# RetNet attention and a gated feed-forward layer on one core: the order of work at the entry of token tile 1, and transposing transfers for chunks 14 to 16

## The chip, the core and the metric

One core of a Trainium2 chip. It has TensorE (PE; its weight loads are shown apart as PEld), VectorE (DVE), ScalarE (ACT), GpSimd (POOL), and SyncE (SP), which here only issues transfers. Sixteen DMA engines move data. PE writes to PSUM, the accumulation memory; DVE and ACT bring results from there to SBUF, the working memory. The metric is device time of one launch in microseconds, the median of several runs; lower is better.

## The reference

Shapes: q, k, v are [8 batches, 8 heads, 576 positions, 64], the feed-forward layer has 4608 tokens (8 x 576), width 512 and 2048 hidden units.

```python
scores = matmul(q, k.T) / sqrt(64)
gamma = 1 - 2 ** (-5 - head)
D[i, j] = gamma ** (i - j) if i >= j else 0
x = matmul(scores * D, v)                 # then [8*576, 512]
h = x @ w_in                              # 512 -> 2048
g = h * tanh(softplus(h))                 # Mish
out = g @ w_out                           # 2048 -> 512
```

## The kernel before

**Chunks and tiles.** The 576 positions of a batch are cut into four chunks of 128 and a rest of 64; two rests make one chunk. There are 36 chunks of 128 tokens. Chunks 0 to 7 are the first 128 positions of the eight batches; 8 to 14 belong to batches 0 and 1 (14 is their two rests), 15 to 21 to batches 2 and 3, and so on. Four chunks make a token tile (t), nine in all. `g1(t, f)` makes 128 of the 2048 hidden units for a tile: four products of 128x512 over `w_in_t` and `xT`, then a Mish activation on ACT into `gT`. `g2(t, i)` does four of the 16 products of one output chunk; `store` copies the result to `res` (DVE or ACT) and SP sends it out.

**Attention.** Decay is put into q, k and v ahead of the products. For a chunk n, `step_p` (P) scales and casts q and k into `qks` on DVE (two instructions of 128x512), `step_v` (V) does the same for v, `step_t` (T) transposes `qks` into `qkT`. For n under NT = 16, T is eight PE transposes into PSUM and copies by ACT; from chunk 16 on it is a transposing transfer (`dma_start_transpose`, L348) on SP's queue, mostly told by `behind` to wait for PE's newest product. `load` brings a chunk's raw q, k and v (`qkraw`, `vraw`) by POOL's queue, into five and seven buffers. `visit(n)` does the rest for the pair n, n+1: states for the next pair (`states`, read from `qks` and `vs`), outputs of this pair (`outputs`, `outputs_end`, which reads `qkT` and the states' cast `ssb`), the next pair's scores (`step_s`, reads the next pair's `qkT`), two casts of `xT` (ACT and DVE, L505), and the masked scores (`step_m`, DVE). State sums are run on DVE a little later (`run(sums)`), their cast to `ssb` on ACT (`run(casts)`).

**The first two tiles** (chunks 0 to 7) go another way, without states: `f_transpose`, `f_scores`, `f_v` (cast of v to `vb`), `f_out` (products, then casts into `xT`). For tile 1 these steps lie among the 16 steps of `g2_first`, the second product of tile 0; `steps` (L712) says at which step T, S, V and O are issued. `vpair` is the raw v of two batches.

**The order** is written out by hand: each engine runs its instructions as the code issues them. The loop over `u` (24 steps) does tile 1's `g1` (steps 0 to 15) and half of its `g2` (16 to 23), with the attention steps of chunks 8 to 13 at the steps that `ps`, `vs` and `ts_` name, and visits to chunks 8 and 10. Then comes the loop over t = 2 to 9 and i = 0 to 15, in which n is the pair visited and w = i % 8 the step; pair 12 is visited at t = 2, i = 6, pair 14 at i = 14. `gated` makes the loads of chunks 17 and 18 wait for an activation of tile 2, `more_loads` makes 19 and 20 wait for PE's newest product. `halved` says for how many of the next products that neither open nor close a sum the 512 columns are done as two products of 256 (L547).

Of the kernel before, what the change touches and what calls it, by code (L numbers as in the profile page):

```python
# [16 lines left out]
def kernel(  # L17
# [21 lines left out]
    P = 128  # L39
# [4 lines left out]
    KC = d_model // P  # L44
    NCH = 4
    NPE = 18
    NT = 16
    NV = 20
    PF = 5

# [10 lines left out]
    N0 = 2 * NCH  # L61
# [38 lines left out]
    fst = {}  # L100
# [71 lines left out]
    xts = {}  # L172
# [65 lines left out]
    def f_out(t, b, copy):  # L238
        if b == 0:
            xts[t] = xp.tile([P, KC, NCH * P], BF16, name="xT")  # L240
        vb = fst[t]["vb"][b]
        if t == 0:
            pool, name = ((ps_h, "hp"), (ps_h, "hp"), (ps_st, "st"), (ps_o, "ops"))[b]
            ot = pool.tile([P, NP, P], F32, name=name)
        else:
            if b % 2 == 0:
                fst[1]["out"] = ps_sc.tile([P, 2, NP, P], F32, name="sc")
            ot = fst[1]["out"][:, b % 2]
        for p in range(NP):
            for e in range(2):  # L250
                nc.tensor.matmul(ot[ds(64 * e, 64), p, :], lhsT=vb[:, 2 * p + e, :],
                                 rhs=fst[t]["sm", b][:, 2 * p + e, :],
                                 start=(p == 0), stop=True, skip_group_check=True)
        if t == 0:
            copy(xts[t][:, :, ts(b, P)], ot)
        elif b % 2:
            for x in range(2):
                copy[x](xts[1][:, :, ts(b - 1 + x, P)], fst[1]["out"][:, x])  # L258

    def f_state(b):  # L260

# [67 lines left out]
    newest = [None]  # L329

    def step_t(n, gate=None):
        flat = live[n]["qks"].rearrange("p i h d -> p (i h d)")
        qk = tr.tile([P, 2, NP, P], BF16, name="qkT", bufs=6)
        if n < NT:
            if n in (N0 + 2, N0 + 4):
# [55 lines left out]
    def written(products):  # L391
        sync = mybir.DependencyInfo(mybir.DependencyClass.Sync, mybir.DependencyReason.DATA)
        seen = nc.sync.nop()
        for ins in products:
            tc.add_manual_dep(seen.ins, ins.ins.name, sync, reason="row halves and a bank")
        return seen
# [64 lines left out]
    def run(jobs, *how):  # L461
        while jobs:
            jobs.pop()(*how)
# [49 lines left out]
    def visit(n, banks, copies, between=None):  # L513


        units, early = states(n + 2)
        if units:
            units[0]()
        both = outputs(n, banks)
        seen = written(outputs_end(n, both, 0))  # L520
        if units:
            step_s(n + 2)
        elif between:
            between()
        for unit in units[1:early]:
            unit()
        outputs_end(n, both, 1, seen)
        for unit in units[max(early, 1):]:
            unit()
        outputs_copy(n, both, copies)  # L530
        if units:
            step_m(n + 2)

    outs = {}
    halved = [0]
    gated = {(2, 0): 17, (2, 1): 18}

# [99 lines left out]
    def att(n, steps):  # L639
        if n >= n_chunks:  # L640
            return
        for step in steps:
            {"P": step_p, "V": step_v, "T": step_t}[step](n)

    dve, act, pool = nc.vector.tensor_copy, nc.scalar.copy, nc.gpsimd.tensor_copy
# [63 lines left out]
        g1(0, f)  # L709
    for i in range(2):  # L710
        f_mix(0, i)
    steps = {0: "T0", 3: "S0 C1", 9: "T1", 11: "S1", 12: "V0 V1 V2 V3", 15: "O0 O1 O2 O3"}  # L712
    for i in range(nF):
        for step in steps.get(i, "").split():
            n = int(step[1])
            if step[0] == "T":
                for j in range(2):
                    f_transpose(1, n, j, [(ps_sc, "sc", (dve, act)[j])])
            elif step[0] == "S":
                f_scores(1, n)  # L720
            elif step[0] == "V":
                f_v(1, n, dve if n == 3 else act)
            elif step[0] == "C":
                for j in range(2):
                    f_mix(n, j)
            else:
                f_out(1, n, (dve, act))
        g2_first(i // 4, i % 4)

    queued = [4 * NCH]  # L730
# [1 line left out]
    def more_loads(upto, gate=None):  # L732
        for _ in range(2):
            if queued[0] <= upto:
                load(queued[0], gate)
                queued[0] += 1


    ps = {0: 0, 4: 1, 8: 2, 11: 3, 18: 5}
    vs = {0: 0, 5: 1, 9: 2, 13: 3, 18: 4, 19: 5}  # L740
    ts_ = {3: 0, 7: 1, 12: 2, 14: 3, 19: 4, 21: 5}
    for u in range(24):
        j, w = divmod(u, 4)
        halved[0] = 2 if 0 < u < 5 else 0
        if u in ps:
            att(N0 + ps[u], "P")
        if u == 11:
            step_m(N0)
        if u in vs:
            att(N0 + vs[u], "V")  # L750
        if w == 0 and j > 0:
            if j < 5:
                load(N0 + j + 3)
            else:
                load(N0 + j + 3)
                queued[0] += 1
        if u == 10:
            units, early = states(N0)
            seen = written(units[0]())
            step_s(N0)  # L760
            units[1]()
            units[2](seen)
            run(sums)
        elif u == 16:
            att(N0 + 4, "P")
        elif u == 17:
            visit(N0, ((ps_o, "ops"), (ps_h, "hp")), (act, act))
            run(sums)
        elif u == 22:
            visit(N0 + 2, ((ps_h, "hp"), (ps_h, "hp")), (act, dve))  # L770
        if u == 20:
            stores(act)
        if u in (13, 20):
            run(casts, dve if u == 13 else act)
        if u in ts_:
            att(N0 + ts_[u], "T")
        stores()
        if u < nF:
            g1(1, u, 2 if u == 0 else 1)
            flush()  # L780
        else:
            g2(1, u - nF)
# [3 lines left out]
    for t in range(2, nT + 1):  # L786
        for i in range(nF):
            n, w = NCH * (t + 1) + i // 8 * 2, i % 8
            if w == 2 and n in cast_at:
                cast_k0(cast_at[n])  # L790
            if w == 2:
                run(casts, act)
                halved[0] = {14: 16, 20: 29}.get(n, 0)
            if w == 6 and n < n_chunks:
                visit(n, ((ps_h, "hp"), (ps_h, "hp")), (act, dve), lambda: g2(t - 1, i))
            if w == 0:
                stores(act if n == N0 + 4 else dve)
                run(sums)
            if w == 7 and n + 2 == NPE:
                stores()  # L800
            if w in (0, 1) and n + 2 < NT:
                att(n + 2 + w, "P")
            if w in ((3, 4) if n + 2 < NPE else (0, 1)):
                att(n + 2 + (w in (1, 4)), "V")
            if w in ((4, 7) if n + 4 <= NPE + 2 else (4, 5)) and n + 4 >= NT:
                stores()
                att(n + 4 + (w != 4), "P")
            if w == 7 and NT <= n + 4 <= NPE + 2:
                step_t(n + 5, newest[0])
            if w in (1, 3) and n + 2 == NT:  # L810
                more_loads(n + 5 + w // 3, newest[0])
            if w == 1 and n + 2 == NPE:
                more_loads(n + 5, newest[0])
            if w == 1 and NPE < n + 2 < n_chunks:
                hold(n + 2)
            if w == 1 and n + 2 >= NPE:
                more_loads(n + 7)
                if t in (3, 4):
                    load_k0(2 * t - 2 + i // 8)
            if w in (4, 5) and n + 2 < NT:  # L820
                att(n - 2 + w, "T")
            stores()


            if t == 2:
                if w == 6:
                    g2(1, 8 + i // 2)
                g1(t, i)
                if w == 6:
                    step_t(n + 4, newest[0])  # L830
                if i % 2 and w != 7:
                    g2(1, 8 + i // 2)
            elif t == nT:
                if i < 12:
                    g2(t - 1, i)
            elif w == 6:

                last = n < n_chunks <= n + 2
                g2(t - 1, i + last)
                g1(t, i)  # L840
                if NPE < n + 4 < n_chunks:
                    for x in ((4, 5) if n + 4 > NPE + 2 else (4,)):
                        step_t(n + x, newest[0])
            elif w == 7 and n < n_chunks <= n + 2:
                g1(t, i)
            elif i % 4 == 0:
                g1(t, i)
                g1(t, i + 1)
                g2(t - 1, i)
            else:  # L850
                if i % 4 != 1:
                    g1(t, i)
                g2(t - 1, i)
# [32 lines left out]
```

## Time and profile before

| what | value |
|---|---|
| median of 3 runs | 299.06 us (298.16 to 299.23) |
| profiled execution, its own time | 297.8 us |
| span of the program in it | 296.1 us |
| busy: PE, DVE, ACT, POOL | 289.9, 140.2, 129.8, 124.9 us |
| transposing transfers (L348) | 20, median 3.2 us from issue to landing |
| loads of raw q, k, v of 256 KB (POOL) | 72, median 6.0 to 6.1 us from issue to landing |

Times in the profile are microseconds from the start of the span. A row of the chain of waits gives a start, a duration and what took it; a row of the timeline gives start, duration, engine, line, operation, tiles and shapes, and in brackets how long the engine stood idle before it and for whom it waited. A row of the list of waits gives total, times and longest. A row for one tile or line gives the minimum, median and maximum duration in ns and the first and last start.

### The profile page before, as it was taken

How to read it: one execution, taken by the hardware profiler on the slowest of the kernel's cores; microseconds unless marked ns; L12 is line 12 of the kernel's file. 1: busy time of each engine (PE TensorE's matmuls, PEld its weight loads, DVE VectorE, ACT ScalarE, POOL GpSimd, SP SyncE). 2: the span in 40 equal slices, each digit the busy share in tenths (PEclk: the TensorE clock that was granted, in tenths of full speed). 3: DMA queues.
4: the chain of work that ended last, by engine and by line, in shares of the span. 5: the costliest groups of instructions: out<-in, count | busy, mean ns of one | idle time of the engine just before them, and what ended most of it. 6: DMA issues, size and time to landing. Idle time of an engine off the chain costs nothing.

```text
span 296.1 us, 7921 instructions
## 1 busy us (share of the span) xinstructions
PE 289.9 (98%) x3479; PEld 156.3 (53%) x3479; DVE 140.2 (47%) x253; ACT 129.8 (44%) x213; POOL 124.9 (42%) x163
## 2 busy tenths in 40 slices
PE   7899999999999999999999999999999999999996
PEld 3556886556456545457645454545454544444443
DVE  6851547497955828454555454535454222010011
ACT  4867126775566534443353534343434433433200
POOL 8945756656427096738392727283020000000000
DMA  7999999999679999798877868686313111010132
GB/s 157 222 202 205 205 239 216 344 222 210 188 164 191 191 227 225 194 238 202 205 201 186 209 137 213 137 205 146 78 54 90 38 38 42 32 35 35 56 88 71
DMA packets 41956, 46.92 MB, mean 158 GB/s; under 512 B 23873, under 2 KB 31041, under 8 KB 41921
## 3 DMA queue, kind: packets, MB, share of 16 engines
q0 software_dynamic: 15120, 31.20, 49.5%
q1 hardware_dynamic: 26656, 15.01, 20.5%
q8 instruction: 27, 0.44, 0.7%
q10 hardware_dynamic: 144, 0.20, 0.2%
q14 instruction: 9, 0.07, 0.1%
HBM read 37.75 MB, written 9.44 MB: 159 GB/s over the span
## 4 chain that ended last, share of the span: by engine, by line
PE 83%; DMA 11%; POOL 3%; DVE 1%; issue 0%; ACT 0%; POOLq 0%; DVEq 0%
PE hp L542 39%; PE ops L542 31%; DMA w_out_t<-in_moe_w_out_dram 4%; DMA vpair<-in_v_dram 4%; DMA w_in_t<-in_moe_w_in_dram 3%; PE hp L547 2%; PE ops L547 2%; PE sc L362 1%; PE hp L493 1%; PE sc L417 1%; PE hp L476 1%; PE hp L623 1%; POOL gT L107 1%; POOL w_in_t L87 1%; PE sc L340 1%; POOL gT L118 1%
## 5 line engine op out<-in xcount | busy, mean ns | idle before, releaser
L542 PE MATMUL hp<-xT,w_in_t 128*128 128x512 bf16 (+1 forms) x539 | 131.0, 376 | 0.7 <-ACT xT L258 0.7
L579 ACT ACTIVATE gT<-hp 128x512 bf16<-128x512 f32 x142 | 84.8, 598 | 94.3 <-PE hp L542 93.5
L542 PE MATMUL ops<-w_out_t,gT 128*128 128x512 bf16 x424 | 104.7, 379 | 0.0
L542 PEld LDWEIGHTS <-w_in_t 128*128 128x128 bf16 x542 | 52.8, 98 | 56.9 <-issue 1.5
L542 PEld LDWEIGHTS <-gT 128*128 128x128 bf16 x478 | 45.5, 98 | 52.2
L631 DVE COPY res<-ops 128x512 f32<-128x512 f32 x28 | 19.3, 690 | 85.2 <-PE ops L542 85.2
L319 DVE TENSOR_TENSOR qks<-qkraw,gqk 128x512 bf16<-128x512 f32 x56 | 36.8, 711 | 2.7 <-DMA qkraw<-in_k_dram 2.7
L297 POOL DMA_DIRECT2D qkraw<-in_q_dram x24 | 21.5, 894 | 17.7 <-PE hp L542 6.3
L326 POOL TENSOR_TENSOR vs<-vraw,gv 128x512 bf16<-128x512 f32 x16 | 16.8, 1069 | 20.1 <-PE hp L476 20.0
L505 DVE CAST xT<-hp 128x512 bf16<-128x512 f32 x13 | 9.0, 692 | 31.6 <-PE hp L493 31.6
L297 POOL DMA_DIRECT2D qkraw<-in_k_dram x24 | 21.4, 891 | 3.9 <-DMA vraw<-in_v_dram 2.1
L297 POOL DMA_DIRECT2D vraw<-in_v_dram x24 | 21.2, 883 | 1.4 <-DMA w_out_t<-in_moe_w_out_dram 0.9
L505 ACT CAST xT<-hp 128x512 bf16<-128x512 f32 x14 | 8.2, 586 | 28.2 <-PE hp L493 28.2
L547 PEld LDWEIGHTS <-gT 128*128 128x128 bf16 x164 | 15.8, 98 | 3.3
L368 DVE TENSOR_TENSOR sm<-sc,mask 128x1024 bf16<-128x1024 f32 x14 | 17.0, 1216 | 0.8 <-PE sc L362 0.8
L453 DVE TENSOR_TENSOR total<-sc,total 128x256 f32<-128x256 f32 x40 | 16.9, 422 | 1.0
L511 POOL COPY held<-qkT 128x1 bf16<-128x1 bf16 x8 | 1.5, 188 | 33.4 <-DMA qkT<-qks 33.4
L456 ACT CAST ssb<-total 128x768 bf16<-128x768 f32 (+3 forms) x13 | 11.6, 894 | 2.9 <-DVE total L453 2.9
L542 PE MATMUL hp<-w_out_t,gT 128*128 128x512 bf16 x52 | 12.7, 379 | 0.0
L547 PE MATMUL hp<-xT,w_in_t 128*128 128x256 bf16 x74 | 12.0, 273 | 0.0
L547 PE MATMUL ops<-w_out_t,gT 128*128 128x256 bf16 x80 | 10.4, 273 | 0.0
L547 PEld LDWEIGHTS <-w_in_t 128*128 128x128 bf16 x76 | 7.4, 98 | 5.4 <-issue 0.2
(130 smaller groups left out, 246.1 us busy)
## 6 DMA issues: line engine op xcount, KB each, us to landing
out_dram<-res SPq DMA_DIRECT2D x31, 256.0 KB, 2.8
qkraw<-in_q_dram POOLq DMA_DIRECT2D x24, 256.0 KB, 6.0
qkraw<-in_k_dram POOLq DMA_DIRECT2D x24, 256.0 KB, 6.0
vraw<-in_v_dram POOLq DMA_DIRECT2D x24, 256.0 KB, 6.1
w_out_t<-in_moe_w_out_dram POOLq DMA_DIRECT2D x4, 512.0 KB, 11.8
gT<-in_k_dram POOLq DMA_DIRECT2D x8, 128.0 KB, 6.4
gT<-in_v_dram POOLq DMA_DIRECT2D x2, 512.0 KB, 6.8
w_in_t<-in_moe_w_in_dram POOLq DMA_DIRECT2D x2, 512.0 KB, 10.8
```

The costliest lines, as they stand in the source:

```text
L87: nc.gpsimd.dma_start(out=w_in_t[:, cs, ds(f0, n)], in_=w_in_r[:, cs, ds(f0, n)])
L297: ins = nc.gpsimd.dma_start(out=t, in_=src[b, :, ds(P * c, P), :].rearrange("h p d -> p h d"))
L319: nc.vector.tensor_tensor(slots[:, :, y], heads[:, :, y], factors[:, :, y].unsqueeze(3).to_broadcast([P, NP, 2, D]), op=OP.mult)
L326: engine.tensor_tensor(vs, live[n]["v"], gv[:, c, :].unsqueeze(2).to_broadcast([P, H, D]), op=OP.mult)
L368: nc.vector.tensor_tensor(sm.rearrange("p e x n i -> p (e x n) i"), live[n]["sc"].rearrange("p e x n i -> p (e x n) i"), mask.unsqueeze(1) ...
L453: nc.vector.tensor_tensor(new[:, k], st[:, j, x], total[b], op=OP.add)
L456: casts.append(lambda copy: copy(lows[:, 0:k], new[:, 0:k]))
L505: copy(xts[t][:, :, ds(P * s, 2 * P)].rearrange("p h (x j i) -> p j h x i", x=2, j=2)[:, j], both[j])
L542: newest[0] = nc.tensor.matmul(to, lhsT=w, rhs=x, start=first, stop=last)
L547: nc.tensor.matmul(to[:, ts(j, n)], lhsT=w, rhs=x[:, ts(j, n)], start=False, stop=False, skip_group_check=True)
L579: done = nc.scalar.activation(gts[t][:, f, :], hp, AX.Mish)
L631: copy(ot, ops)
```

## The change

In tile 1 the casts of v for batches 2 and 3 are issued at step 15, just ahead of the output products, and not at step 12 with the other two. The four casts of `xT` (128x512, DVE and ACT by turns) become two of 128x1024: ACT takes batches 0 and 1, DVE takes 2 and 3.

NT becomes 14, so chunks 14 and 15 are no longer transposed by PE and ACT but by transfers, as is 16. Their P and T move ahead: chunk 14 has P at u = 21 and T at u = 22, behind the visit; chunk 15 has both at u = 23; chunk 16 has both at i = 1 of tile 2 (before: P at i = 4, T at i = 6). None of the three waits for a product of PE. Chunk 17's stay at i = 7. The loads of chunks 17 and 18 wait for the activations of f = 2 and 3 of tile 2 and not of 0 and 1; those of 19 and 20 are issued at i = 10 and 12 and not at 9 and 11. From i = 2 of tile 2 on, 16 more products are done in halves. SP's queue gets two transfers more; POOL's order is the same.

```diff
-    NT = 16
+    NT = 14
...
         elif b % 2:
-            for x in range(2):
-                copy[x](xts[1][:, :, ts(b - 1 + x, P)], fst[1]["out"][:, x])
+            copy(xts[1].rearrange("p h (b i) -> p b h i", i=P)[:, ds(b - 1, 2)], fst[1]["out"])
...
-    gated = {(2, 0): 17, (2, 1): 18}
+    gated = {(2, 2): 17, (2, 3): 18}
...
-    steps = {0: "T0", 3: "S0 C1", 9: "T1", 11: "S1", 12: "V0 V1 V2 V3", 15: "O0 O1 O2 O3"}
+    steps = {0: "T0", 3: "S0 C1", 9: "T1", 11: "S1", 12: "V0 V1", 15: "V2 V3 O0 O1 O2 O3"}
...
-                f_out(1, n, (dve, act))
+                f_out(1, n, (act, dve)[n // 2])
...
-    ps = {0: 0, 4: 1, 8: 2, 11: 3, 18: 5}
+    ps = {0: 0, 4: 1, 8: 2, 11: 3, 18: 5, 21: 6, 23: 7}
...
             visit(N0 + 2, ((ps_h, "hp"), (ps_h, "hp")), (act, dve))
+            att(N0 + 6, "T")
+        elif u == 23:
+            att(N0 + 7, "T")
...
-                halved[0] = {14: 16, 20: 29}.get(n, 0)
+                halved[0] = {12: 16, 14: 16, 20: 29}.get(n, 0)
...
-            if w in (0, 1) and n + 2 < NT:
-                att(n + 2 + w, "P")
...
+            if n == 12 and w == 1:
+                att(n + 4, "PT")
-            if w in ((4, 7) if n + 4 <= NPE + 2 else (4, 5)) and n + 4 >= NT:
+            if w in ((4, 7) if n + 4 <= NPE + 2 else (4, 5)) and (n > 12 or w == 7):
                 stores()
                 att(n + 4 + (w != 4), "P")
-            if w == 7 and NT <= n + 4 <= NPE + 2:
+            if w == 7 and n + 4 <= NPE + 2:
                 step_t(n + 5, newest[0])
-            if w in (1, 3) and n + 2 == NT:
-                more_loads(n + 5 + w // 3, newest[0])
+            if w in (2, 4) and n + 4 == NPE:
+                more_loads(n + 5 + w // 4, newest[0])
...
-            if w in (4, 5) and n + 2 < NT:
-                att(n - 2 + w, "T")
...
-                if w == 6:
+                if w == 6 and n > 12:
                     step_t(n + 4, newest[0])
```

## The prediction

> **What bounds the kernel now.** I read the page's busy shares and chain first, then the chain of waits, in order of time, around the places that the diff touches, and then the timeline of each engine there.
>
> ```profile
> span 296.1 us, 7921 instructions
> PE 289.9 (98%) x3479; PEld 156.3 (53%) x3479; DVE 140.2 (47%) x253; ACT 129.8 (44%) x213; POOL 124.9 (42%) x163
> PE 83%; DMA 11%; POOL 3%; DVE 1%; issue 0%; ACT 0%; POOLq 0%; DVEq 0%
> ```
>
> PE is busy for 98% and carries 83% of the chain; the other engines are under half. So a microsecond counts only if PE waits for it or works in it. The list of waits has one wait of PE for another engine after the start:
>
> ```profile
> PE hp L542 <- ACT xT L258: 0.7, 1, 0.7
> ```
>
> It is the entry into tile 1, and the chain shows what stands before it:
>
> ```profile
> 32.47 12.47 DMA vpair<-in_v_dram
> ...
> 45.06 0.43 DVE vb L233
> 45.49 1.20 DVE res L631 x2
> 46.68 0.61 DVE xT L258
> ...
> 47.32 0.59 ACT xT L258
> ...
> 48.55 0.81 PE hp L542 x5
> ...
> 50.99 0.45 PE sc L340 x8
> ```
>
> The load of v for batches 6 and 7 lands at 44.94 (32.47 + 12.47). DVE then makes vb of batch 3, copies two finished rows of results that were queued behind it, casts a first row quarter of xT, ACT casts the next, and only then does PE begin tile 1. From there on PE has a fixed stream of work: what is taken out of it, or what lets it begin earlier, moves the end.
>
> **Part 1, the order in tile 1.** V2, V3 move from step 12 to step 15, and four xT casts of 128x512 become one of 128x1024 on ACT (batches 0, 1) and one on DVE (batches 2, 3). The timeline there (start, duration, engine, line):
>
> ```profile
> 41.72 2.36 DVE L226 TENSOR_TENSOR sm<-sc,dmask 128x1024 bf16<-128x1024 f32 x2 [1.45 <-PE sc L219]
> ```
> ```profile
> 45.02 0.62 ACT L233 CAST vb<-vpair 128x512 bf16<-128x512 f32 x1 [1.48 <-DMA vpair<-in_v_dram]
> 45.54 0.58 ACT L631 COPY res<-hp 128x512 f32<-128x512 f32 x1
> ```
> ```profile
> 44.90 0.38 PE L542 MATMUL ops<-w_out_t,gT 128*128 128x512 bf16 x1
> 45.20 1.12 PE L251 MATMUL sc<-sm,vb 128*64 128x128 bf16 x32
> 46.26 0.83 PE L547 MATMUL st<-w_out_t,gT 128*128 128x256 bf16 x6
> ...
> 47.95 1.41 PE L542 MATMUL hp<-xT,w_in_t 128*128 128x256 bf16 x9 [0.65 <-ACT xT L258]
> ```
> ```profile
> L205 DVE COPY qkT<-sc x2: 1225/1225/1225, 29.6 to 39.0; 128x1024 bf16<-128x1024 bf16 x2
> L205 ACT COPY qkT<-sc x2: 1012/1012/1012, 30.0 to 39.5; 128x1024 bf16<-128x1024 bf16 x2
> ```
>
> After the change: DVE is free at 44.08 and does the first result row at once; the second starts when its products end (44.90 + 0.38 = 45.28) and holds DVE for 0.60 (1.20 for two) before the next; V3 comes third, 45.93 to 46.36. ACT copies its result row before 45.02, does V2 from 45.02 to 45.64 as now, and the first pair's cast from about 45.9 (O0 and O1 are the first half of the 45.20 row) to 46.9 by the 1.01 us row. On PE, O2 runs at 45.65, O3 waits for V3 until 46.42, runs 0.24 (a quarter of 1.06, the distance from 45.20 to 46.26) and leaves 0.1 for the change of shape, then the seven products on st, which last 0.87 (six halves of 0.109 and one of 0.216, rows below): 47.64. The first half of g1(1,0) then needs no wait and goes at 47.64 instead of 47.95. The second half waits for DVE's pair: O3 done and visible at 46.9, plus 1.23, is 48.15 against 48.55 now. Gain 0.40, and about 0.1 more because the first activation of tile 1 is no longer behind a late result copy: 0.5. Bounds: 0 if the wait merely moves to O3, and 0.98 if all that PE stands there goes (47.13 to 47.95, and 0.16 ahead of 48.55). DVE ends its casts at 48.1 against 47.9, so chunk 8's scaling starts 0.2 later; its reader, the transposes at 50.99 (then 50.5), leaves more than a microsecond.
>
> **Part 2, chunks 14 to 16.** PE loses 16 transposes; 16 products get a second half.
>
> ```profile
> 80.98 0.45 PE sc L340 x8
> ...
> 82.29 0.45 PE sc L340 x8
> ...
> 86.64 3.45 PE hp L542 x16
> ...
> 139.31 1.53 PE ops L547 x14
> ```
>
> The transposes cost PE 0.45 + 0.45 = 0.90 on the path, with products on both sides. A product is 3.45/16 = 0.216, a half 1.53/14 = 0.109: two halves cost 0.218, so 16 products cost 0.04 more. PE's instruction count stays the same. Net 0.86. ACT loses two 1.01 us copies, which nothing waited for: nothing gained.
>
> The row prices a 128-column transpose at 56 ns. The Trainium skill ("TensorE: Matmul & The Clock Gate", section on sustained spacing) gives about 81 ns per matmul at N = 128 in a stream with weight loads; by that the removed work would be 1.30 and the time 0.4 lower. The trace does not agree (0.45 for eight), so the row is used.
>
> What must now be on time. P14 and P15 move to steps 21 and 23, P16 and T16 to the second step of tile 2:
>
> ```profile
> 71.14 1.29 DVE L326 TENSOR_TENSOR vs<-vraw,gv 128x512 bf16<-128x512 f32 x2
> 74.08 0.69 DVE L505 CAST xT<-hp 128x512 bf16<-128x512 f32 x1 [1.65 <-PE hp L493]
> 74.69 1.22 DVE L368 TENSOR_TENSOR sm<-sc,mask 128x1024 bf16<-128x1024 f32 x1
> 75.82 1.33 DVE L453 TENSOR_TENSOR total<-sc,total 128x256 f32<-128x256 f32 x3
> ...
> 77.53 2.49 DVE L319 TENSOR_TENSOR qks<-qkraw,gqk 128x512 bf16<-128x512 f32 x4
> ```
>
> P14 (half of 2.49, 1.25) fits the 1.65 that DVE stands idle before the cast at 74.08. P15 goes between sm and the sums and pushes these by 1.25, to 77.0 less the 0.5 of part 1; their cast for ACT then starts near 78.0, ends at 78.8, just when ACT's next activation is due (79.29 less 0.5). Cost nothing, with no slack; without that cover it would be tenths. The transfers:
>
> ```profile
> DMA to landing us min/median/max: 3.0/3.2/6.6
> ```
> ```profile
> 89.58 10.89 SPq L348 DMA_TRANSPOSE qkT<-qks  x2
> ```
> ```profile
> L362 PE MATMUL sc<-qkT x32: 186/194/194, 84.9 to 85.2; 64*64 64x64 bf16 x32
> ```
> ```profile
> L362 PE MATMUL sc<-qkT x32: 186/194/194, 96.6 to 96.9; 64*64 64x64 bf16 x32
> ```
>
> T14 is issued at about 73.2, T15 after P15 at 76.7. Both are first read in the visit to chunks 12 and 13, now at 84.9, then at 83.5: T15 has 6.8 and needs 3.0 to 6.6. On SP's queue the next store stands behind T15's wait, some 1.3 us; result tiles have four buffers, so nobody waits. T16 goes at 79.8 instead of after 87 and is read at 95.2, as is T17. The loads of 17 and 18 wait for two more activations, those of 19 and 20 for one more step:
>
> ```profile
> 77.95 0.88 POOL L297 DMA_DIRECT2D qkraw<-in_q_dram  x1 [5.89 <-ACT gT L579]
> ...
> 89.53 0.88 POOL L297 DMA_DIRECT2D qkraw<-in_q_dram  x1 [6.32 <-PE hp L542]
> ```
> ```profile
> 87.99 1.28 DVE L319 TENSOR_TENSOR qks<-qkraw,gqk 128x512 bf16<-128x512 f32 x2
> ```
> ```profile
> DMA to landing us min/median/max: 5.2/5.8/6.2
> ```
> ```profile
> DMA to landing us min/median/max: 8.9/9.8/12.4
> ```
>
> (The last two are the raw loads issued from 77.9 to 83 and from 34 to 58.) Load 17 starts 12 products later, 77.95 + 2.59 - 0.5 = 80.0, its k part at 80.9, landing at 86.1 to 87.1. P17, on DVE at 87.99 now, is due at 86.6: at most 0.5 late. T17 follows at 88.2 to 88.7; with 3.0 to 6.6 it lands at 91.2 to 95.3, for a use at 95.2. Today's T17 is issued at 89.58, 0.05 after load 19 began; then load 19 begins at 89.53 + 1.73 - 1.4 = 89.9, so T17 has over a microsecond alone. I take it as on time. POOL has nothing but later loads behind these waits.
>
> **Sum.** -0.50 - 0.90 + 0.04 = -1.36, against the profiled execution's 297.8 (span 296.1): 296.4. The median of the runs shown is 299.06, 1.26 above it; carried over, 297.7. PE's stream after 48 us is fixed, so I put the 1.26 mostly ahead of it, into the loads. If v lands d later, today's second half of g1(1,0) slips by d; in the new order V3 slips only once d passes 0.87 (46.36 against 45.49 + d). The gain of part 1 then grows to 1.3. Between 0.5 and 1.3 I take 0.65: 297.5.
>
> **Rivals.**
> 1. Tile 1 gives nothing, because O3 and the longer casts eat it, and PE enters the second half at 48.5 as now. For it: DVE's single cast is 1.23 long and starts after V3. Time: 299.06 - 0.86 = 298.2.
> 2. Slower: load 17's landing decides. P17, its transfer and the visit at 95.2 hang on it. With a landing time of 9.3 (rows: 5.2 to 6.2 there, 8.9 to 12.4 when the queue was deep) k is there at 90.2, T17 is issued at 91.8 and lands at 98.4 by 6.6: PE stands 3.2, time 300.7; with 12.4, 303.8. It costs something from 6.2 on if T17 takes its longest, and turns the sign once PE stands 1.6. For it: T16 now shares the engines with these loads. Against: the highest row there is 6.2.
> 3. T15 is late at 83.5, for loads 15 and 16 still land beside T14. From a landing time of 6.8 on each microsecond is one of PE; at 10 it is 3.2, time 300.7. Against: 6.6 is the maximum of 20. The Trainium skill ("VectorE: DVE Perf Modes", rules for kernel authors) prefers TensorE for a 128x128 transpose where PSUM will do, 390 ns against 1309 ns by DMA, which speaks against this part; taken one after the other, eight such would take an estimated 10.5 us and give this rival. The trace shows 3.0 to 6.6 for all eight.
>
> **How the numbers follow.** A change under 0.5% (1.5 us) is about what can't be told from none. Forecast with its own range 296.9 to 298.2: 0.60, of which 0.43 lie under 297.56 (faster) and 0.17 within. Rival 1: 0.17, the same. Rival 2: 0.15, of which 0.10 slower (over 300.56) and 0.05 the same, stalls that only eat the gain. Rival 3: 0.08, 0.06 slower, 0.01 the same, 0.01 still faster. Faster 0.44, same 0.40, slower 0.16. The range reaches from 296.4 (299.06 less 1.3 and 0.86, less half of the 1.07 between the highest and the lowest run shown) to 299.6 (no change, and the same half more), which leaves out the 0.16 of the slower cases.
>
> **What would show it.** Right: xT casts of 128x1024, one on ACT, one on DVE, side by side; PE's second half of tile 1 near 48.1; no L340 group at 81 and 82; halves of 0.109 in their place; the visits that stand at 84.4 and 96.1 now begin 1.4 earlier with no wait of PE in front of the qkT reads. Wrong: PE or its weight loads waiting for the transfer of qks into qkT, P17 on DVE waiting for the load of k, ACT's cast of the sums holding up an activation, or a longer standstill of PE between O2 and O3 than 0.5.

## The result, and the profile after

The changed kernel takes 297.27 us (median of 16 runs, 297.08 to 298.65); the kernel before, timed beside it, 298.64 (16 runs, 298.00 to 299.23). The ratio is 0.9962, with a 95% interval from 0.9952 to 0.9971: 1.13 us less (0.87 to 1.43). The forecast was 297.5.

The profiled execution of the changed kernel happens to be the slowest of its runs, 298.65: everything in it starts late, so its times are compared here from a common point and not from the start of the span. Lines behind 257 have a number one lower than before (L541 is the old L542). The head of the page, with the shares of the chain by engine:

```profile
span 296.9 us, 7883 instructions
PE 286.4 (96%) x3440; PEld 157.0 (53%) x3479; DVE 140.9 (47%) x252; ACT 128.2 (43%) x210; POOL 124.4 (42%) x163
PE 89%; DMA 6%; issue 2%; POOL 1%; DVE 0%; POOLq 0%
```

PE still carries the chain. Of its 3479 matmuls 39 have no record here (the weight loads are all there); each leaves a hole in the rows below, "issue" of 0.05 behind a half and of 0.16 behind a whole product. They aren't waits.

**Tile 1.** The chain of waits of the changed kernel (start, duration, what), and the timeline of PE and rows of L257:

```profile
46.55 0.23 PE ops L541
46.78 0.02 issue
46.80 0.07 DVE res L630
46.87 0.54 issue
47.41 0.43 DVE vb L233
47.84 0.04 issue
47.88 0.41 PE sc L251 x8
48.29 0.76 PE st L546 x6
49.05 0.05 issue
49.11 1.32 PE hp L541 x9
```
```profile
46.69 0.86 PE L251 MATMUL sc<-sm,vb 128*64 128x128 bf16 x24
47.88 0.41 PE L251 MATMUL sc<-sm,vb 128*64 128x128 bf16 x8 [0.33 <-DVE vb L233]
```
```profile
L257 ACT CAST xT<-sc x1: 1012/1012/1012, 47.4 to 47.4; 128x1024 bf16<-128x1024 f32 x1
L257 DVE CAST xT<-sc x1: 1225/1225/1225, 48.3 to 48.3; 128x1024 bf16<-128x1024 f32 x1
```

The output products begin at 46.69, 1.49 later than before (45.20). V3 is held by DVE's second result copy, which waits for PE's product; O3 then waits for V3; after that PE goes on with no wait over 0.1, and the 0.65 before the first half of `g1(1,0)` is gone. That first half begins 2.42 after the first output product (before: 47.95 - 45.20 = 2.75), the second half, inside the group of nine, at 49.62, 2.93 after it (before 3.35).

**Chunks 14 to 16.** The chain of the two kernels at the visits to chunks 10 and 12, before and after:

```profile
72.77 0.25 PE sc L417 x16
...
84.46 0.15 PE st L417 x2
```
```profile
74.12 0.25 PE sc L416 x16
...
79.74 0.22 PE hp L541
79.96 0.44 PE hp L546 x4
...
84.96 0.15 PE st L416 x2
```

From visit to visit it was 11.69 and is 10.84: 0.85 less. The transposes at L340 (now L339) are gone there, halves stand in their place. The transfers of chunks 14 to 17 (issued from 75.1 to 89.8) and the q, k, v loads issued from 81.9 to 91.8 landed in time:

```profile
L347 SPq DMA_TRANSPOSE qkT<-qks x4: 1240/1292/1363, 75.1 to 89.8; - x4
DMA to landing us min/median/max: 4.8/5.1/5.5
```
```profile
DMA to landing us min/median/max: 4.5/7.1/7.3
```

Their readers stand at 85.6 and 97.3, and no wait of PE or of its weight loads for `qkT` is in the list.

**What was not in the sum: the end.** The last store, and the first and last drain of SP's queue behind it (before, then after):

```profile
293.54 0.33 SPq L627 DMA_DIRECT2D out_dram<-last  x1
...
L881 SPq DRAIN  x3: 7/7/13, 295.2 to 295.5; - x3
```
```profile
294.04 0.33 SPq L626 DMA_DIRECT2D out_dram<-last  x1
...
L881 SPq DRAIN  x3: 7/7/13, 296.1 to 296.4; - x3
```

From the issue of the last store to the drain it was 1.7 and is 2.1. The store takes the same 1.54 to land. Between lie SP's waits for the completion semaphores of the transfers, one after another, about 0.06 each. An instruction of this kind has its record when its wait has ended; the starts of these records:

```
before  store lands 295.08; waits end at 293.92 293.97 294.03 294.10 294.16 294.22 294.28 294.77 | 295.10 295.16, drain 295.22
after   store lands 295.58; waits end at 294.42 294.47 | 295.60 295.66 295.72 295.78 295.84 295.90 295.96 296.02, drain 296.09
```

Before, the last store holds up the ninth of ten waits, and one is left when it has landed. After, it holds up the third, and seven are left. From landing to drain that is 0.14 against 0.51. In all 14 profiles of this study it is 0.14 without the new transfers and 0.51 with them: a fixed 0.37 that part 2 loses again. That two transfers more on SP's queue move the last store to another semaphore of a rotating set is the reading that fits; the set itself isn't in the profile.

**And a scatter that both kernels have.** In the visit to chunk 8 PE stands between products with nothing to wait for:

```profile
67.57 0.14 PE sc L361 x17
67.71 0.16 issue
67.88 0.32 PE sc L361 x15
```

From the last product before to the first after, 0.36 are lost here, 0.07 before, and 0.77 in a second profile of the changed kernel; experiments 11 and 12 come back to it.

### The profile page after: what moved, and what is told of

Its sections match the earlier page's. It is cut to its first block, busy times and chain, and to the rows that moved or that the text cites. A ratio compares the mean times of both kernels' runs of the same rounds, so it can differ in the third digit from the quotient of the medians.

```text
span 296.9 us, 7883 instructions
## 1 busy us (share of the span) xinstructions
PE 286.4 (96%) x3440; PEld 157.0 (53%) x3479; DVE 140.9 (47%) x252; ACT 128.2 (43%) x210; POOL 124.4 (42%) x163
## 4 chain that ended last, share of the span: by engine, by line
PE 89%; DMA 6%; issue 2%; POOL 1%; DVE 0%; POOLq 0%
PE hp L541 40%; PE ops L541 30%; PE hp L546 5%; PE ops L546 4%; DMA w_in_t<-in_moe_w_in_dram 3%; DMA gT<-in_v_dram 3%; PE sc L361 1%; PE hp L492 1%; PE sc L416 1%; PE hp L475 1%; PE hp L622 1%; PE st L546 1%; POOL gT L107 1%; PE st L416 1%; PE sc L339 1%
## 5 line engine op out<-in xcount | busy, mean ns | idle before, releaser
L541 PE MATMUL hp<-xT,w_in_t 128*128 128x512 bf16 (+1 forms) x512 | 127.6, 376 | 1.0 <-DMA w_in_t<-in_moe_w_in_dram 0.2
L541 PE MATMUL ops<-w_out_t,gT 128*128 128x512 bf16 x403 | 99.9, 379 | 2.0 <-issue 1.9
L541 PEld LDWEIGHTS <-w_in_t 128*128 128x128 bf16 x534 | 52.0, 98 | 55.4 <-DMA w_in_t<-in_moe_w_in_dram 1.2
L541 PEld LDWEIGHTS <-gT 128*128 128x128 bf16 x470 | 44.8, 98 | 51.3
L546 PEld LDWEIGHTS <-gT 128*128 128x128 bf16 x180 | 17.3, 98 | 3.6
L546 PE MATMUL hp<-xT,w_in_t 128*128 128x256 bf16 x90 | 14.4, 273 | 0.0
L546 PE MATMUL ops<-w_out_t,gT 128*128 128x256 bf16 x96 | 12.4, 273 | 0.2
L546 PEld LDWEIGHTS <-w_in_t 128*128 128x128 bf16 x92 | 9.0, 98 | 6.3 <-issue 0.2
L541 PE MATMUL hp<-w_out_t,gT 128*128 128x512 bf16 x49 | 12.0, 379 | 0.2 <-issue 0.2
## 6 DMA issues: line engine op xcount, KB each, us to landing
w_out_t<-in_moe_w_out_dram POOLq DMA_DIRECT2D x4, 512.0 KB, 11.8
```

The source lines that it names most:

```text
L541: newest[0] = nc.tensor.matmul(to, lhsT=w, rhs=x, start=first, stop=last)
L546: nc.tensor.matmul(to[:, ts(j, n)], lhsT=w, rhs=x[:, ts(j, n)], start=False, stop=False, skip_group_check=True)
```

## The experiments

Each kernel was run beside the kernel before on the same chip; the ratio is to that kernel. All compute the whole result.

**1. The order alone (part 1).** The kernel before with:

```diff
-            for x in range(2):
-                copy[x](xts[1][:, :, ts(b - 1 + x, P)], fst[1]["out"][:, x])
+            copy(xts[1].rearrange("p h (b i) -> p b h i", i=P)[:, ds(b - 1, 2)], fst[1]["out"])
...
-    steps = {0: "T0", 3: "S0 C1", 9: "T1", 11: "S1", 12: "V0 V1 V2 V3", 15: "O0 O1 O2 O3"}
+    steps = {0: "T0", 3: "S0 C1", 9: "T1", 11: "S1", 12: "V0 V1", 15: "V2 V3 O0 O1 O2 O3"}
...
-                f_out(1, n, (dve, act))
+                f_out(1, n, (act, dve)[n // 2])
```

> The kernel before with the new order of tile 1 alone (V2, V3 at step 15, two wide casts); transposes of chunks 14 and 15 stay on PE. Theory (the gains of the two parts add up, and tile 1 is worth the 0.4 us that the aligned profiles show): 0.4 to 0.6 us faster, ratio 0.9980 to 0.9987. Rival (tile 1 gives nothing, the whole gain is the transposes): 0 us. Rival (v lands late in most runs, so the order is worth up to 1.3): over 0.9 us, ratio under 0.9970. In the profile PE should stand about 0.5 us ahead of the last eight output products and not at the entry of tile 1.

Measured: 298.00, ratio 0.9986 (0.9974 to 0.9997), 0.42 us less (0.09 to 0.78).

**2. The transfers alone (part 2).** The changed kernel with those three places as they were before.

```diff
-            copy(xts[1].rearrange("p h (b i) -> p b h i", i=P)[:, ds(b - 1, 2)], fst[1]["out"])
+            for x in range(2):
+                copy[x](xts[1][:, :, ts(b - 1 + x, P)], fst[1]["out"][:, x])
...
-    steps = {0: "T0", 3: "S0 C1", 9: "T1", 11: "S1", 12: "V0 V1", 15: "V2 V3 O0 O1 O2 O3"}
+    steps = {0: "T0", 3: "S0 C1", 9: "T1", 11: "S1", 12: "V0 V1 V2 V3", 15: "O0 O1 O2 O3"}
...
-                f_out(1, n, (act, dve)[n // 2])
+                f_out(1, n, (dve, act))
```

> The changed kernel with the old order of tile 1 (old V steps, four narrow casts). Theory: 0.86 us faster than before (16 transposes of 0.056 less, 16 products in halves for 0.04), ratio 0.9971. Rival (the transfers make PE or its copies wait, so that the order of tile 1 brought the gain): under 0.4 us. The distance on PE from the end of the visit to chunks 10 and 11 to the start of the visit to 12 and 13 shrinks by 0.86.

Measured: 298.08, ratio 0.9991 (0.9980 to 1.0003), 0.27 less (0.60 less to 0.09 more). From chunk 10 to 12 it takes 10.84 as in the changed kernel, so the gain on PE is there (0.85); 0.37 of it are lost at the end. The 0.48 left over lies inside the interval, 0.85 does not. From the second half of `g1(1,0)` to the issue of the last store this profile has 244.19, the kernel before 244.99. The two parts alone add up to 0.69 and together measured 1.13; the intervals allow for that, and no run places the difference.

**3 and 4. The two halves of part 1.** The kernel before with the wide casts alone, and with the late V2 and V3 alone:

```diff
-            for x in range(2):
-                copy[x](xts[1][:, :, ts(b - 1 + x, P)], fst[1]["out"][:, x])
+            copy(xts[1].rearrange("p h (b i) -> p b h i", i=P)[:, ds(b - 1, 2)], fst[1]["out"])
...
-                f_out(1, n, (dve, act))
+                f_out(1, n, (act, dve)[n // 2])
```

> The kernel before with the two wide casts alone; V2 and V3 stay at step 12. By the rows of before: output products 45.20 to 46.16, st products to 47.13, ACT's cast of batches 0 and 1 46.1 to 47.1 behind its result copy, DVE's of 2 and 3 46.65 to 47.9 behind its two. The second half of the first product of tile 1 at 47.95 against 48.55: 0.6 us faster if v lands as in that profile. Rival (the gain in tile 1 comes from V2 and V3 no longer standing ahead of the result copies): 0 to 0.2 us.

```diff
-    steps = {0: "T0", 3: "S0 C1", 9: "T1", 11: "S1", 12: "V0 V1 V2 V3", 15: "O0 O1 O2 O3"}
+    steps = {0: "T0", 3: "S0 C1", 9: "T1", 11: "S1", 12: "V0 V1", 15: "V2 V3 O0 O1 O2 O3"}
```

> The kernel before with V2 and V3 at step 15 alone; the four narrow casts stay, and ACT's still wait for DVE's. Theory: V3 ends at 46.36, DVE casts batch 0 until 46.97, ACT batch 1 until 47.6, then batch 2 by DVE and batch 3 by ACT until 48.2: 0.3 us faster. Rival (the late V is what gives the gain in tile 1): 0.5 us, as much as both edits.

Measured: wide casts alone 297.56, ratio 0.9973 (0.9960 to 0.9987), 0.81 less; late V alone 298.32, ratio 0.9997 (0.9986 to 1.0009), no difference that can be told (0.3 was expected and lies inside the interval). The wide casts carry the gain of part 1: alone they are 0.39 ahead of both edits, with intervals that overlap. With them alone PE does not stop between the output products (chain of that kernel):

```profile
45.39 1.01 PE sc L251 x32
46.40 0.76 PE st L546 x6
47.16 0.21 PE st L541
47.38 0.44 PE hp L541 x4
47.82 0.03 issue
47.84 0.81 PE hp L541 x5
```

The profiles taken together show why the late V adds little to that. Times of the load of v, of the first output product and of the second half of `g1(1,0)`:

| kernel | v landed | first output product | second half | behind v | behind the product |
|---|---|---|---|---|---|
| before | 44.94 | 45.20 | 48.55 | 3.61 | 3.35 |
| 2, old order | 45.38 | 46.20 | 48.99 | 3.61 | 2.79 |
| changed | 46.16 | 46.69 | 49.62 | 3.46 | 2.93 |
| 6, 7, 8 below, new order | 45.11, 45.13, 45.03 | 45.44, 45.61, 45.59 | 48.36, 48.53, 48.51 | 3.25 to 3.48 | 2.92 |
| 1, new order, v late | 45.55 | 45.22 | 48.26 | 2.71 | 3.04 |
| 5 below, two profiles, new order | 45.37, 44.98 | 45.59, 46.20 | 48.55, 49.35 | 3.18, 4.37 | 2.96, 3.15 |
| changed, second profile | 45.82 | 45.87 | 49.00 | 3.18 | 3.13 |
| 4, late V alone | 45.06 | 45.56 | 48.57 | 3.51 | 3.01 |
| 3, wide casts alone | 44.91 | 45.32 | 47.84 | 2.93 | 2.52 |

In the old order the second half follows v, 3.61 behind it in both profiles. In the new one it follows PE's own product where v is early, since V3 stands behind a copy that needs that product: by 2.92 to 2.96, and by 3.13 and 3.15 in the two second profiles, in which V3 took 0.64 and 0.66 and not 0.43. Early V3 with wide casts is 0.4 better there. So what part 1 is worth depends on the execution. In that of experiment 1, v landed after PE had arrived: the old order would have given 45.55 + 3.61 = 49.16 there, against 48.26; of these 0.9 the wide casts alone would give 0.7 by their own row (45.55 + 2.93 = 48.48), the late V 0.2. In that of experiment 2, PE itself arrived 1.0 later and v 0.4 later than before: there the old order's 2.79 is even shorter than the new one's 2.92.

**5. No halves.**

```diff
-                halved[0] = {12: 16, 14: 16, 20: 29}.get(n, 0)
+                halved[0] = {14: 16, 20: 29}.get(n, 0)
```

> The changed kernel without the 16 products in halves in tile 2 (32 PE instructions fewer). Theory (halves only cost 2 ns each): 0.04 us faster than the changed kernel, which can't be told from it, so 1.1 to 1.4 us faster than before. Rival (the halves keep PE's instruction stream where it was, and without them PE stands somewhere for its instructions, as it does for 0.3 us in the visit to chunks 8 and 9 of the changed kernel's profile): 0.3 us or more slower than the changed kernel, with new gaps on PE that no semaphore ends.

Measured: 298.30, ratio 0.9997 (0.9984 to 1.0011). The visits are 10.80 apart, not 10.84, so the halves cost the 0.04 of the sum; yet without them the kernel loses the whole gain. To find where, the same kernel was profiled a second time (12).

**6. The loads of chunks 17 to 20 where they were before.**

```diff
-    gated = {(2, 2): 17, (2, 3): 18}
+    gated = {(2, 0): 17, (2, 1): 18}
...
-            if w in (2, 4) and n + 4 == NPE:
-                more_loads(n + 5 + w // 4, newest[0])
+            if w in (1, 3) and n + 4 == NPE:
+                more_loads(n + 5 + w // 3, newest[0])
```

> The changed kernel with the loads of chunks 17 to 20 as early as before. Theory (the transfers have several microseconds to spare): no difference from the changed kernel, under 0.1 us, though the transfers of 15 and 16 land 1 to 2 us later than now (they have 4.9 and 5.5 from issue to landing in the changed kernel's profile, and 15 is read about 2 us after it lands). Rival (the later loads are needed): PE waits for the transfer of chunk 15 in the visit to chunks 12 and 13, 0.3 us or more slower than the changed kernel.

Measured: 306.06, ratio 1.0262 (1.0239 to 1.0284), 7.8 us more: the rival came out, but at chunks 16 and 17 and not at 15, and far larger. Chunk 16's transfer (issued at 80.11) and chunk 17's (89.75) took 13.4 and 15.0 us to land. The rows of the transfers, the chain, and two stretches (length, busy time and count of PE, PEld, DVE, ACT and POOL, granted clock of PE, share of the DMA engines' time, GB/s), and then the first of these stretches in the changed kernel:

```profile
DMA to landing us min/median/max: 13.4/14.2/15.0
```
```profile
89.75 14.99 DMA qkT<-qks
104.74 0.04 issue
104.78 0.43 PE sc L361 x12
...
105.64 1.82 PE ops L541 x4
```
```profile
84.00:92.00 8.00, 6.94 (x126) 3.76 (x112) 5.41 (x9) 3.70 (x6) 2.05 (x3) 1.00 1.12 89
...
104.00:106.00 2.00, 1.22 (x50) 0.88 (x51) 0.32 (x1) 0.28 (x1) 0.00 (x0) 0.50 0.68 207
```
```profile
84.00:92.00 8.00, 7.84 (x165) 4.69 (x166) 5.78 (x10) 4.29 (x7) 3.41 (x5) 1.00 1.01 223
```

Where the transfer of chunk 16 meets the loads, the DMA engines are no less busy (1.12 against 1.01) but move 89 GB/s in place of 223, and the loads are drawn out as well: those issued from 79.7 to 82.3 took 12.9 to 13.3 us. By the DMA records, the packets of the two kinds lie side by side there from 80 to 93; in the changed kernel they lie mostly one behind the other (SP's queue alone from 79 to 84, the loads alone from 86 to 91). Why chunk 17's transfer in the kernel before, which also met a load, needed only 6.6 us, stays open. PE stands 7.6 us for chunk 17's transfer, and then its granted clock is 0.50: four products take 1.82, or 0.455 each, where the row of before has 0.216.

The Trainium skill ("Advanced Engine Details and Errata", section on the X-bar transpose) says that transposing transfers are as fast as regular ones on this chip. This case's trace agrees where their packets hardly meet those of the loads (4.8 to 5.5 us in the changed kernel, beside 4.5 to 7.3 for the loads of 256 KB); side by side with those loads it does not, at 89 GB/s and 13.4 to 15.0 us.

**7. Those loads two products later.**

```diff
-    gated = {(2, 2): 17, (2, 3): 18}
+    gated = {(2, 4): 17, (2, 5): 18}
```

> The changed kernel with the loads of chunks 17 and 18 behind the activations of f = 4 and 5 of tile 2 (2.6 us later again). This is rival 2 of the prediction, made on purpose: the k part of chunk 17 lands at about 90.8 on the scale of the changed kernel's profile (88.2 there), its scaling on DVE is due at 88.5 there, so 2.4 late, the transfer of 17 then issued at 92.3 and landing at 97.5 by its 5.2, for a use at 97.1: PE stands 0.4 us or more, and the state sums behind it on DVE hold ACT's cast for as long. 0.3 to 1.5 us slower than the changed kernel. Rival (there was slack everywhere): no difference.

Measured: 298.88, ratio 1.0024 (1.0009 to 1.0038), 0.7 more than before and 1.8 more than the changed kernel. The chain, and the list of waits:

```profile
91.54 6.50 DMA qkT<-qks
98.04 0.04 issue
98.08 0.32 PE sc L361 x16
```
```profile
PE hp L541 <- ACT gT L578: 0.9, 1, 0.9
```

Chunk 17's k landed at 90.09, its transfer was issued at 91.54 and landed at 98.04, 0.5 after PE needed it; and PE waited 0.9 for an activation that stood behind ACT's cast of the sums. This is rival 2, brought about by the later loads, and with it the sign that the prediction named for it: the cast of the sums holding up an activation.

**8. Only chunks 17 and 18 early.**

```diff
-    gated = {(2, 2): 17, (2, 3): 18}
+    gated = {(2, 0): 17, (2, 1): 18}
```

> The changed kernel with only the loads of 17 and 18 as early as before; 19 and 20 stay late. With all four early the run was 7.8 us slower: the transfer of 16, issued at 80.1 behind 14 and 15 and beside load 17, took 13.4 us to land, that of 17 beside load 19 took 15.0. Theory (each transfer that meets a load of raw data behind other transfers is drawn out): the transfer of 16 takes over 10 again, that of 17, which now starts ahead of load 19, less, and PE waits less: 1 to 5 us slower than the changed kernel. Rival (loads 19 and 20 alone do it): as the changed kernel.

Measured: 300.41 (297.68 to 301.73 in five runs), ratio 1.0076 (1.0053 to 1.0099). Its profile is of the fastest of these runs, 297.68, and has no wait worth naming: chunk 16's transfer took 11.8 us there and still came in time. So the loss in the others isn't seen in a trace; that a longer landing of that kind makes it is argued, not shown. This is 3.4 us more than the changed kernel by the ratios, and 5.6 less than with all four early: the places of 17 and 18 and those of 19 and 20 both matter.

**9. V3 ahead of the second result copy.** From the changed kernel:

```diff
-    steps = {0: "T0", 3: "S0 C1", 9: "T1", 11: "S1", 12: "V0 V1", 15: "V2 V3 O0 O1 O2 O3"}
+    steps = {0: "T0", 3: "S0 C1", 9: "T1", 11: "S1", 12: "V0 V1", 14: "V3", 15: "V2 O0 O1 O2 O3"}
```

> The changed kernel with V3 at step 14, ahead of DVE's second result copy and not behind it. In the changed kernel's profile v lands at 46.16, the copy starts at 46.80, V3 at 47.41 and PE stands 0.49 us ahead of the last output products. With V3 first it is done at 46.7, PE does not stand, the copy ends at 47.4, DVE casts batches 2 and 3 from 47.5 to 48.7, and the second half of tile 1's first product goes at 48.75 instead of 49.62. Theory: 0.5 to 0.9 us faster than the changed kernel, 1.6 to 2.2 faster than before, less where v lands late. Rival (the wide cast by DVE sets the second half anyway): under 0.2 us faster.

Measured: 296.91 (296.79 to 297.24), ratio 0.9955 (0.9943 to 0.9967). The second half begins 2.56 behind the first output product, not 2.92. The lowest median here, 1.34 us under the kernel before, where 1.6 to 2.2 were expected; its interval overlaps that of the changed kernel.

**10. Part 2 with the wide casts, V's as before.** From the changed kernel:

```diff
-    steps = {0: "T0", 3: "S0 C1", 9: "T1", 11: "S1", 12: "V0 V1", 15: "V2 V3 O0 O1 O2 O3"}
+    steps = {0: "T0", 3: "S0 C1", 9: "T1", 11: "S1", 12: "V0 V1 V2 V3", 15: "O0 O1 O2 O3"}
```

> The changed kernel with V2 and V3 back at step 12: wide casts and transfers without the late V. Wide casts alone gave 0.83 us against before and both edits 0.42; the aligned profiles put the second half of tile 1's first product 2.52 after the start of the output products with wide casts alone, 3.04 and 2.93 with both. Theory (late V is a loss while v lands by 45, and the parts add): 1.6 to 1.7 us faster than before, ratio 0.9944, 0.4 to 0.6 better than the changed kernel and level with V3 ahead of the copy (0.9955). Rival (late V pays in most runs, as the prediction put it with v landing later than in the profile): no better than the changed kernel's 0.9962.

Measured: 297.23, ratio 0.9959 (0.9946 to 0.9973): level with the changed kernel, as the rival had it; the theory's 0.9944 lies outside the interval. Its profile has the second half 2.40 behind the first output product, the shortest of all, in an execution in which v was 1.34 early. That this 0.5 is missing from the median is not settled; executions in which v lands later would do it, as the table above has it.

**11 and 12. Two second profiles,** of the changed kernel and of the one without halves, with no edit.

> The changed kernel once more, for a second profile. In the visit to chunks 8 and 9 PE stands 0.36 us in the middle of the scores in its first profile, and 0.07 to 0.77 in the others, 1.4 to 1.7 us after the end of a 16 KB packet of the instruction queue. Theory A (how late that packet is differs between executions): another length here, by more than 0.1. Theory B (it belongs to the kernel): 0.3 to 0.4 again. The interval from the output products of tile 1 to the second half of its first product stays at 2.9 us, the one from the visit to chunk 10 to that to chunk 12 at 10.84.

> The changed kernel without the 16 halves once more, for a second profile. Its first shows the visit to chunk 12 0.04 earlier behind that to chunk 10 (10.80 against 10.84), as priced, and no gap that the halves would close, but 0.77 us of standing in the visit to chunks 8 and 9, which lies ahead of them. Theory A (that standing differs between executions, not kernels): another length here. Theory B (the kernel without halves has it in every execution, and this is the 1 us by which its median is behind the changed kernel): 0.7 to 0.8 again.

Measured: one run each, 298.45 and 299.51. The second profile without halves has a hole that the first has not; the chain, and the DMA queues from 155 to 158.7 (queue, packets, MB, share):

```profile
157.72 0.02 PE st L416 x2
157.74 0.91 issue
158.64 0.22 PE sc L416 x2
```
```profile
q8 instruction: 1, 0.02, 2.6%
```

For 1.07 us PE has nothing to do in the middle of a group of 64x64 products and waits for no semaphore. A packet of 16 KB of the instruction queue is on its way just then. The same pair, a packet and a hole, stands in all 14 profiles, each time in the visit to chunk 8 and three times in a later one (us):

| kernel, visit | packet ends | visit begins | PE goes on | behind the packet's end | lost |
|---|---|---|---|---|---|
| before, 8 | 65.02 | 65.80 | 66.52 | 1.50 | 0.07 |
| 1, order alone, 8 | 64.86 | 65.50 | 66.26 | 1.40 | 0.10 |
| 2, transfers alone, 8 | 65.45 | 66.24 | 67.02 | 1.57 | 0.12 |
| 3, wide casts alone, 8 | 64.47 | 65.09 | 66.19 | 1.72 | 0.44 |
| 4, late V alone, 8 | 65.62 | 65.81 | 67.24 | 1.62 | 0.77 |
| changed, 8 | 66.23 | 66.86 | 67.88 | 1.65 | 0.36 |
| changed, second profile, 8 | 66.07 | 66.25 | 67.67 | 1.60 | 0.77 |
| 5, no halves, 8 | 65.61 | 65.79 | 67.22 | 1.61 | 0.77 |
| 5, the visit at 156 | 155.54 | 155.89 | 157.19 | 1.65 | 0.10 |
| 5, second profile, 8 | 65.96 | 66.60 | 67.68 | 1.72 | 0.42 |
| 5, second profile, the visit at 156 | 157.22 | 156.35 | 158.64 | 1.42 | 1.07 |
| 6, loads early, 8 | 64.84 | 65.60 | 66.53 | 1.69 | 0.27 |
| 6, visit to 12 | 84.17 | 83.54 | 85.65 | 1.48 | 1.25 |
| 7, loads later, 8 | 65.64 | 65.78 | 67.15 | 1.51 | 0.71 |
| 8, 17 and 18 early, 8 | 65.24 | 65.75 | 66.75 | 1.51 | 0.34 |
| 9, V3 first, 8 | 64.43 | 65.31 | 66.14 | 1.71 | 0.17 |
| 10, late V left out, 8 | 65.77 | 66.21 | 67.26 | 1.49 | 0.39 |

PE goes on 1.4 to 1.7 us behind the end of the packet, wherever it is, and tends to lose more where the packet ends later: over 1 us where it ends inside the visit, 0.71 to 0.77 where it ends less than 0.2 ahead of it, 0.07 to 0.44 where it ends 0.35 to 0.88 ahead. The reading that fits is that it waits for its instructions: in a visit it gets through them far faster than elsewhere (32 products of 64x64 in 0.27 us, where a whole product takes 0.216). So the hole belongs to the execution as well as to the kernel: 0.36 and 0.77 in the changed one, as theory A had it. The other expectation of experiment 11 missed by 0.2: from the first output product to the second half it is 3.13 in the second profile and not 2.9.

In the changed kernel the packet near 157 runs from 151.04 to 151.96, without the halves from 154.35 in one execution and 155.67 in the other, up to or into the visit at 156. The 16 halves put back the 16 instructions that part 2 takes out, and with them the refills behind stay where they were. That this is what makes experiment 5 a whole gain slower is argued, not shown: it rests on these two profiles, and the first of them lost only 0.1 there.

The Trainium skill ("Runtime: NRT & Kernel Launch", section on instruction fetch) has the refill in blocks of 16 KiB and calls the cost of crossing one mostly hidden. The trace agrees on the size of the packets, and on most of the 27 in an execution; ahead of or in a burst of short matmuls it shows 0.07 to 1.25 us lost each.

## Why the prediction was right, point by point

- **What bounds it.** Right: PE's stream, and what holds up its entry into tile 1. Set back by the 1.49 that its first output product is late, the profile gives 49.62 - 1.49 = 48.13 for the second half, forecast 48.15, and 47.62 for the first, forecast 47.64. PE stands before O3 for V3, as the bound named.
- **The step from the profile to the median failed.** Part 1 was taken at 0.65: 0.40 from the rows, 0.1 for the first activation of tile 1, and 0.15 because v was thought to land later in the median run. Part 1 alone brought 0.42 (0.09 to 0.78), as much as the 0.40. The 0.1 stands in no wait: once PE has entered tile 1, the list of waits before has no wait of PE for another engine. The 0.15 took v to be late and PE not. Experiment 1's execution was of that kind (v late, 0.9); in the other profiles v lands ahead of the first output product, and where PE is late too, as in experiment 2, the new order gains nothing.
- **Which piece of part 1 works.** The forecast gave the credit to both. Late V puts V3 behind a copy that waits for PE. Wide casts alone brought 0.81 against 0.42 for both, and with the transfers, experiment 10, they are level with the changed kernel: late V is not needed, and whether it costs anything in the median is not settled.
- **Transposes and halves.** 0.86 forecast, 0.85 measured. The row of 56 ns per transpose was the right price.
- **The sum lacked two terms.** The 0.37 at the end, found in every kernel with the transfers, is the one that was taken at nothing (two transfers more on SP's queue). The other is the refill of instructions, up to a microsecond per place; the prediction noted that PE's instruction count stays the same and gave that no price. It shows in the visits to chunks 12 and 14: forecast 1.4 earlier, they begin 0.99 earlier from the common point (84.89 - 1.49 = 83.40 against 84.39). That is the 0.42 of the entry and the 0.85, less the 0.29 that this execution lost in the visit to chunk 8 over and above the kernel before.
- **Why 297.5 came out all the same.** In part this is luck. The gains that were measured, 0.42 and 0.85, less the 0.37, make 0.90, inside the measured 0.87 to 1.43. The forecast took off 1.51 (0.65 and 0.86), 0.6 too much, but from a median of three runs, 299.06, which is 0.42 above that of 16. The measured 297.27 is lower still: from median to median the change is 1.37, by the ratio 1.13. Both profiles of the changed kernel are of executions above its median (298.65 and 298.45), with 0.36 and 0.77 lost in the visit to chunk 8, so what the median execution has in place of that isn't seen.
- **"Nothing waits."** Right for this change. P14 and P15, and the cast of the sums with the activation behind it, in the timelines of DVE and ACT:

```profile
73.70 1.29 DVE L318 TENSOR_TENSOR qks<-qkraw,gqk 128x512 bf16<-128x512 f32 x2
...
77.20 1.28 DVE L318 TENSOR_TENSOR qks<-qkraw,gqk 128x512 bf16<-128x512 f32 x2
```
```profile
79.77 0.83 ACT L455 CAST ssb<-total 128x768 bf16<-128x768 f32 x1 [0.26 <-DVE total L452]
80.65 0.60 ACT L578 ACTIVATE gT<-hp 128x512 bf16<-128x512 f32 x1
```

  The cast ends as the activation starts: no slack, as forecast. Chunk 17's k landed at 88.21, 86.7 in the forecast's time (86.1 to 87.1), and its transfer at 95.05 for a use at 97.3.
- **The rivals.** Tile 1 giving nothing did not come. Load 17 late (2) and transfers late beside loads (3) did not come either, but both are real: two products later costs 0.7 over the kernel before, and the old places cost 7.8. Rival 3 had the mechanism and put it at chunk 15; it sits at chunks 16 and 17, and its size, 13 to 15 us to land, was above the 10 that it reckoned with. Moving the loads was priced as a cost of timing; without it part 2 loses 7.8 us.

## What to carry to other kernels

Before a transposing transfer is put in the place of PE transposes, look at which loads are on the DMA engines while it lands, and move them apart first; the landing time of transfers that met no loads is no price for one that does. When instructions are taken out of an engine that is always busy, look at where its instruction packets fall against its bursts of short instructions, since everything behind may move. And with a gain under a microsecond, read several profiles from a common point: one execution's entry into a stage depends on a load that lands somewhere else in the next, and a hole of 0.07 to 0.77 us stands in the same place of every one of them.

## What the runs showed of the hardware that was not expected

- A transposing transfer beside the loads of raw q, k and v: 89 GB/s at a DMA share of 1.12, and 13.4 to 15.0 us to land. In the changed kernel, where they hardly meet, it takes 4.8 to 5.5 us, and in the same stretch the loads move 223 GB/s at 1.01.
- PE seems to run out of instructions: in 17 places it stood without a semaphore to wait for, went on 1.4 to 1.7 us behind the end of a 16 KB packet of the instruction queue, and lost 0.07 to 1.25 us, the same kernel 0.36 once and 0.77 once.
- The end of a kernel is not free: SP's waits for completion semaphores take 0.06 each, and which of them the last store holds up went with 0.37 more in ten profiles of ten.
- After standing for 7.6 us PE went on at a granted clock of 0.50.
